# Linear-attention sums as phi(k)^T (x, 1), turned by DMA, in a kernel of two attention heads on one core

## The chip, the core and the metric

The kernel runs on one core of a Trainium2 chip. The metric is the device time of one execution in microseconds; the time of a kernel is the median of several runs. Engines are called by the names of the profile: PE (TensorE), DVE (VectorE), ACT (ScalarE), POOL (GpSimd) and SP (SyncE, which here issues every DMA). One hardware profile shows one execution, and "L287" in it is line 287 of the kernel.

## The reference, cut to what matters

Two independent blocks, A and B, on x of 2048 tokens by D = 640, with H = 32 heads of 20. A is attention over a sliding window of 256 keys. B is linear attention; the change concerns B alone:

```python
phi = lambda t: jnp.where(t > 0, t + 1, jnp.exp(t)) + 1e-6
pq, pk = phi(q), phi(k)
kv = jnp.einsum("bhsd,bhse->bhde", pk, v)
z = jnp.einsum("bhsd->bhd", pk)
num = jnp.einsum("bhqd,bhde->bhqe", pq, kv)
den = jnp.einsum("bhqd,bhd->bhq", pq, z)[..., None] + 1e-6
o = num / den        # then o @ wo; the outputs of A and B stand side by side
```

All is in bf16, with sums in f32.

## The kernel before, in words

Tokens are taken in NS = 4 blocks of SB = 512, features in KT = 5 blocks of P = 128.

**A** sets the beat. Its work is cut into 76 "tiles". A tile is a set of score products (`scores`, L763, matmul at L773) into one PSUM tile of four banks, one exponential of all of it on ACT (L793), masks on POOL (L814), and, two tiles later, the products with the values (`values`, L825, matmul at L841), whose result DVE transposes (L854), inverts (L865) and multiplies into a buffer N (L871). N has one buffer for all four blocks of tokens; four DMA transposes (`turn`, L882) carry it to oT, and the first write of the next block's N waits for them.

**B and the projections of A fill the gaps.** All other work stands as generators that yield the number of columns that each matmul streams. A plan, written by hand, gives each piece a time in tiles (`at(t0, t1, generator, n)` for chains of products, `do` for single actions), and the pieces run in the order of these times. FILL is the sum of the columns of all fill work; from it each tile gets a credit, and `take` draws that many columns of fill work between scores and values. Dense products go through four PSUM banks (`bank`, L276); `evac` (L266, its copies at L272 and L274) gives each evacuation to ACT or DVE, whichever a running account says has less to do. `soon(fn, n)` (L247) puts an action (mostly the issue of a DMA) off until n more banks have begun; `later` does so with the second half of phi on DVE (L301 and L304; its exponential on ACT is L297); chains of products (`chain`) have their matmul at L287.

**B, step by step**, with what the change touches:
- `load_tok` (L545) loads x by rows, [token, 640], into a tile of the pool `rows` (two buffers). `b_keys` (L532) makes phi(k) of 512 tokens by rows, `pk`.
- `b_sums(half)` (L550, matmul at L556) sums over the keys of half the tokens (8 blocks of 128). Because kv needs v = x wv, it suffices to know G = x^T phi(k) and to multiply by wv afterwards. x is the stationary operand, phi(k) streams. For each of 5 blocks of x's features: 8 products of 512 columns; then 5 x 8 products of 128 columns for the last 128 features of phi(k); last, z, the plain sum of phi(k): 5 x 8 products with phi(k) stationary and one column of ones streaming. The first half goes to G_acc and z_acc in f32, the second is added to it on DVE (L570 for G, L601 for z) and stored in bf16: G straight into the weights' tile `wB`, z into `zk`.
- `b_kv` (L628, matmul at L635) multiplies wv by G, by groups of six heads; `kv_ready` (L621) masks zk and kv on POOL so that each head meets its own rows alone; `b_merge` (L654, matmul at L663) multiplies kv by wo.
- `b_q(s)` (L677) makes phi(q), transposed to rows by DMA (`tok`, L694, also in the pool `rows`); `b_den(s)` (L699, L706) makes the denominators; `quotients(s)` (L732) queues four divisions on DVE (L742), each followed by a DMA transpose to `xA` (L746); one is taken a tile, by `quotient()`, in tiles that have no values, or when more than two are due, or past tile URGENT; `b_out(s)` (L750) multiplies the result by the merged matrix, after all its quotients.
- The last block of A closes the kernel: `turn_last` (L903, matmul transposes at L908, copied to oT at L914 and L916) and `a_out_last` (L918). Between the two stands what is left of the fill, the end of `b_out(3)`.

SP issues DMAs strictly in the order in which the program names them, and an issue waits on SP for what it needs.

Of the kernel before, what the change touches and what calls it, by code (L numbers as in the profile page):

```python
# [9 lines left out]
P = 128  # L10
ALU = mybir.AluOpType
ACT = mybir.ActivationFunctionType
ENG = mybir.EngineType
BF16 = mybir.dt.bfloat16
# [6 lines left out]
SB = 512  # L21
TPS = SB // P

FILL = 390760
TAIL = 13000

VALUES = 2200
TILE = 3000
COPY = 160
AHEAD = 600  # L30
URGENT = 70

# [70 lines left out]
def kernel(  # L103
# [10 lines left out]
    nc = tc.nc  # L114
    _, S, D = A_x.shape
    KT = D // P
# [13 lines left out]
    wp = pool("weights", 1)  # L130
# [10 lines left out]
    rp = pool("rows", 2)  # L141
    op = pool("o", 2)
# [9 lines left out]
    for n in "AB":  # L152
# [65 lines left out]
    NHC = GH + 2  # L218
# [28 lines left out]
    def soon(fn, banks):  # L247
        posts.append((begun[0] + banks, fn))
        posts.sort(key=lambda p: p[0])
# [16 lines left out]
    def evac(dst, src, n=SB, to=None):  # L266

        if to is None:
            to = "A" if load["A"] < load["D"] + AHEAD else "D"
        load[to] += n + COPY  # L270
        if to == "A":
            nc.scalar.activation(out=dst, in_=src, func=ACT.Copy)  # L272
        else:
            nc.vector.tensor_copy(out=dst, in_=src)  # L274

    def bank(wide=False):  # L276
        flush(begun[0] - 2)
        begun[0] += 1
        settle(False)
        if wide:  # L280
            return dps.tile([P, 2 * SB], BF16, name="dense")
        return dps.tile([P, SB], F32, name="dense")
# [49 lines left out]
    for c in range(KT):  # L332
        m = EXTRA * c
        while m < EXTRA * (c + 1):
            n = min(EXTRA * (c + 1) - m, DH - m % DH)
# [128 lines left out]
        nc.gpsimd.memset(t[:, VW:], 0.0)  # L464
    for t in v_bufs:
        nc.gpsimd.memset(t[:, :, :, DH:HV], 1.0)
    ones = wp.tile([P, 1], BF16, name="ones")
    nc.gpsimd.memset(ones[:], 1.0)
    nc.gpsimd.memset(wo_sb["B"][:, KT, :], 0.0)

    def a_v(s):
# [69 lines left out]
        yield from tok_rows(xB[s], w_sb["B"], D, done)  # L541

    x_tok = {}

    def load_tok(s):  # L545
        x_tok[s] = rp.tile([P, TPS, D], BF16, name="tok")
        src = xsrc["B"][s * SB : (s + 1) * SB, :].rearrange("(t p) d -> p t d", p=P)
        nc.sync.dma_start(out=x_tok[s], in_=src)

    def b_sums(half):  # L550
        flush()
        blocks = [(x_tok[s], pk_of[s], tb) for s in (2 * half, 2 * half + 1) for tb in range(TPS)]

        def product(out, lhs, rhs, n):
            for i, (x, pk, tb) in enumerate(blocks):
                nc.tensor.matmul(  # L556
                    out,
                    lhsT=lhs(x, pk)[:, tb, :],
                    rhs=rhs(pk, tb),
                    start=(i == 0),  # L560
                    stop=(i == len(blocks) - 1),
                )
                if i < len(blocks) - 1:
                    yield n

        def keep(at, src, n):
            if half == 0:
                evac(G_acc[at], src, n)
            else:
                nc.vector.tensor_tensor(out=G[at], in0=src, in1=G_acc[at], op=ALU.add)  # L570

        def rows(c):
            return lambda x, pk: x[:, :, c * P : (c + 1) * P]

        every = slice(None)
        for c in range(KT):
            ps = bank()
            yield from product(ps[:], rows(c), lambda pk, tb: pk[:, tb, 0:SB], SB)
            keep((every, c, slice(0, SB)), ps[:], SB)
            yield End(SB)  # L580
        for cs in (range(0, KT - 1), range(KT - 1, KT)):
            ps = bank()
            pv = ps[:].rearrange("p (c n) -> p c n", n=P)[:, 0 : len(cs), :]
            for i, c in enumerate(cs):
                yield from product(pv[:, i, :], rows(c), lambda pk, tb: pk[:, tb, SB:D], P)
                yield P
            zv = ps[:, P : P + KT]
            if len(cs) == 1:
                for c in range(KT):
                    yield from product(  # L590
                        zv[:, c : c + 1],
                        lambda x, pk: pk[:, :, c * P : (c + 1) * P],
                        lambda pk, tb: ones[:],
                        60,
                    )
            keep((every, slice(cs[0], cs[-1] + 1), slice(SB, D)), pv, len(cs) * P)
            if len(cs) == 1 and half == 0:
                nc.vector.tensor_copy(out=z_acc[:], in_=zv)
            elif len(cs) == 1:
                heads = [P, KT, NHC]  # L600
                nc.vector.tensor_tensor(  # L601
                    out=zk[:, :, :, 0],
                    in0=zv.unsqueeze(2).to_broadcast(heads),
                    in1=z_acc[:].unsqueeze(2).to_broadcast(heads),
                    op=ALU.add,
                )
            yield End(60)

    def own_heads(sgn):

# [10 lines left out]
    def kv_ready(step):  # L621

        if step == 0:
            keep_own_head(zk[:], 0, NHC, 1)
        else:
            own_heads(3 - 2 * step)

    def b_kv():  # L628

        for gs in (range(0, 4), range(4, NGR)):  # L630
            ps = bank()
            for i, g in enumerate(gs):
                w = min(GD, D - g * GD)
                for kt in range(KT):
                    nc.tensor.matmul(  # L635
                        ps[0:w, i * GD : i * GD + w],
                        lhsT=w_sb["B"][:, kt, 2 * D + g * GD : 2 * D + g * GD + w],
                        rhs=G[:, kt, g * GD : g * GD + w],
                        start=(kt == 0),
                        stop=(kt == KT - 1),  # L640
                    )
# [35 lines left out]
    def b_q(s):  # L677
        quotient(s - 2)
        xt = xB[NS + s]
        pq = pqp.tile([P, KT, SB], BF16, name="phi")  # L680
        pq_of[s] = pq
        tok = rp.tile([P, TPS, D], BF16, name="tok")
        tok_of[s] = tok
        for c in range(KT):
            ps = bank()
            yield from chain(
                ps[:],
                lambda kt: w_sb["B"][:, kt, c * P : (c + 1) * P],
                lambda kt: xt[:, kt, :],
                SB,  # L690
            )

            def to_tokens(c=c):
                nc.sync.dma_start_transpose(out=tok[:, :, c * P : (c + 1) * P], in_=pq[:, c, :])  # L694

            phi(pq[:, c, :], ps[:], then=lambda fn=to_tokens: soon(fn, 2))
            yield End(SB)
# [34 lines left out]
    def quotients(s):  # L732


        def one(tb):
            settle()
            add_load(d=1400)
            if tb == 0:
                oT_B[s] = xp.tile([P, KT, SB], BF16, name="xA")
            v = tok_of[s][:, tb, :]  # L740
            vh = v.rearrange("p (h e) -> p h e", e=DH)
            nc.vector.tensor_tensor(  # L742
                out=vh, in0=vh, in1=rden_of[s][:, tb, :, :].to_broadcast([P, H, DH]), op=ALU.mult
            )
            out = oT_B[s][:, :, tb * P : (tb + 1) * P]
            soon(lambda: nc.sync.dma_start_transpose(out=out, in_=v), 1)  # L746

        quotients_due.extend((s, tb, one) for tb in range(TPS))
# [272 lines left out]
    def at(t0, t1, gen, n):  # L1021
        for i in range(n):
            plan.append((t0 + (i + 0.5) / n * (t1 - t0), gen, i == n - 1))

    def do(t0, t1, fns):
        fns = list(fns)
        for i, fn in enumerate(fns):
            plan.append((t0 + (i + 0.5) / len(fns) * (t1 - t0), None, fn))
# [24 lines left out]
        at(t0, t1, b_sums(half), KT + 2)  # L1053
    for s, t in ((0, 6), (1, 11), (2, 24.2), (3, 28.2)):
        do(t, t, [lambda s=s: load_tok(s)])
    at(40.4, 42, b_kv(), 2)
    do(42.8, 44.8, [lambda c=c: kv_ready(c) for c in range(3)])
    for s, tq, td, tx in ((0, (39.5, 45), 46.3, 46.8), (1, (45, 50), 53, 54.3),
                          (2, (52, 57), 59.4, 60.4), (3, (58.6, 62.4), 64.9, 65.4)):
        at(*tq, b_q(s), KT)  # L1060
        at(td, td + 0.1, b_den(s), 1)
        do(tx, tx, [lambda s=s: quotients(s)])
# [102 lines left out]
```

## Time and profile before

| what | us |
|---|---|
| median of 3 runs (257.19 to 257.9) | 257.81 |
| the profiled execution, its own time | 259.17 |
| span of the profile, first to last instruction | 257.4 |
| busy: PE / ACT / DVE / POOL | 251.1 / 200.0 / 178.3 / 171.4 |
| granted PE clock | 1.000 of full speed |

The profiled execution took 1.8 us more than its span (what lies around the program), and 1.4 us more than the median. In rows of the timeline the columns are start, duration, engine, line, operation, out<-in and count; an entry in brackets is idle time of that engine before it and who ended it. A row of the waits reads "who <- for whom: total us, times, longest". A row of the windows gives the length of the stretch, then the busy time of PE, PE's weight loads, DVE, ACT and POOL (instructions in brackets), the PE clock, and the DMAs' share and rate. In the view by source line the figures are durations in ns, shortest/median/longest.

### The profile page before, as it was taken

What the parts mean: (1) busy time and instruction counts of PE and PEld (TensorE: products, weight loads), DVE (VectorE), ACT (ScalarE), POOL (GpSimd) and SP (SyncE); (2) the same over time, 40 slices, a digit from 0 to 9 for tenths busy, and PEclk for the clock granted to TensorE, in tenths of its full rate; (3) what the DMA queues carried; (4) which work ended last, traced back from release to release, by engine and by line L of the source; (5) the groups of instructions that cost most, each with busy time, mean ns of one, the idle gap of its engine ahead of it and who ended that gap; (6) DMA issues with size and microseconds to landing.
All of it is one profiled execution on the core that took longest, in us unless ns stands there. A gap on an engine that the chain in (4) does not pass through costs nothing.

```text
span 257.4 us, 10670 instructions
## 1 busy us (share of the span) xinstructions
PE 251.1 (98%) x4705; PEld 144.9 (56%) x4705; DVE 178.3 (69%) x308; ACT 200.0 (78%) x260; POOL 171.4 (67%) x211
## 2 busy tenths in 40 slices
PE   8899999999999999999999999999999999999985
PEld 7544445556556745455457655556556555555663
DVE  0345787787845456867655698599999879969552
ACT  3366888898767788897677888888889998988642
POOL 7123778876794856758495787949677695968600
PEclk9999999999999999999999999999999999999999
DMA  6997569699743152993544393642858599473905
GB/s 206 295 229 188 106 177 122 130 275 194 100 85 40 36 198 34 229 277 109 114 124 120 72 181 45 167 48 57 199 89 154 155 124 178 94 178 65 238 29 187
DMA packets 65012, 36.35 MB, mean 141 GB/s; under 512 B 48197, under 2 KB 63941, under 8 KB 64965
## 3 DMA queue, kind: packets, MB, share of 16 engines
q1 hardware_dynamic: 64965, 35.67, 64.3%
q8 instruction: 37, 0.61, 1.0%
q14 instruction: 10, 0.08, 0.1%
HBM read 14.42 MB, written 9.83 MB: 94 GB/s over the span
## 4 chain that ended last, share of the span: by engine, by line
PE 93%; DMA 5%; SPq 0%; ACT 0%; DVE 0%; issue 0%; ACTq 0%
PE dense L287 52%; PE S_ps L773 11%; PE dense L556 10%; PE dense L841 9%; PE dense L422 8%; DMA wA<-in_A_wqkv_dram 3%; DMA xA<-tok 2%; PE dense L663 1%; PE dense L706 1%; PE dense L635 1%; PE dense L188 0%; DVE wB L274 0%; SPq L968 0%; ACT vA L272 0%; SPq L182 0%
## 5 line engine op out<-in xcount | busy, mean ns | idle before, releaser
L793 ACT ACTIVATE p<-S_ps 128x2048 bf16<-128x2048 f32 x76 | 142.3, 1872 | 30.7 <-PE S_ps L773 29.6
L814 POOL TENSOR_SCALAR_AFFINE_SELECT p<-p 128x512 bf16<-128x512 bf16 (+1 forms) x152 | 122.8, 831 | 62.9 <-ACT p L793 60.5
L287 PE MATMUL dense<-xA,wqk 128*128 128x512 bf16 x200 | 50.0, 380 | 0.0
L814 POOL TENSOR_SCALAR_AFFINE_SELECT plow<-p 128x1024 bf16<-128x1024 bf16 x32 | 40.2, 1255 | 0.0
L773 PEld LDWEIGHTS <-kpad 20*128 20x128 bf16 (+1 forms) x1664 | 20.1, 97 | 26.7 <-issue 25.1
L773 PE MATMUL S_ps<-qpad,kpad 20*128 20x64 bf16 (+3 forms) x1664 | 34.5, 211 | 0.0
L854 DVE STREAM_TRANSPOSE T<-dense 128x512 f32<-128x512 f32 x32 | 22.8, 712 | 11.2 <-PE dense L841 11.1
L287 PEld LDWEIGHTS <-wqk 128*128 128x128 bf16 x200 | 18.5, 98 | 20.6 <-issue 1.3
L301 DVE TENSOR_SCALAR e<-e 128x512 bf16<-128x512 bf16 x40 | 22.5, 564 | 10.7 <-ACT e L297 9.9
L422 PE MATMUL dense<-wA,xA 128*128 128x320 bf16 x160 | 28.0, 302 | 1.1 <-DMA wA<-in_A_wqkv_dram 1.1
L304 DVE SCALAR_TENSOR_TENSOR phi<-dense,e 128x512 bf16<-128x512 f32 x40 | 27.7, 692 | 1.5
L841 PE MATMUL dense<-p,vA 128*32 128x64 bf16 (+2 forms) x1152 | 26.2, 222 | 0.0
L287 PE MATMUL dense<-wB,xB 128*128 128x512 bf16 (+1 forms) x160 | 25.9, 300 | 0.0
L287 PE MATMUL dense<-xB,wB 128*128 128x512 bf16 x100 | 25.8, 380 | 0.0
L297 ACT ACTIVATE e<-dense 128x512 bf16<-128x512 f32 x40 | 23.4, 593 | 2.9 <-PE dense L287 2.6
L287 PE MATMUL dense<-wo,oT 128*128 128x512 bf16 (+2 forms) x160 | 25.3, 300 | 0.3 <-DVE wB L274 0.3
L556 PE MATMUL dense<-phi,tok 128*128 128x512 bf16 (+1 forms) x160 | 25.1, 300 | 0.0
L287 PE MATMUL dense<-wB,xA 128*128 128x512 bf16 (+1 forms) x160 | 24.1, 300 | 0.8 <-DMA xA<-tok 0.8
L841 PEld LDWEIGHTS <-vA 128*32 128x32 bf16 x1664 | 21.6, 96 | 2.7 <-issue 0.7
L422 PEld LDWEIGHTS <-xA 128*128 128x128 bf16 x160 | 14.6, 98 | 10.0 <-issue 2.5
L272 ACT ACTIVATE osb<-dense 128x512 bf16<-128x512 f32 (+1 forms) x25 | 13.9, 571 | 7.1 <-PE dense L287 7.1
L871 DVE TENSOR_TENSOR N<-T,recA 128x320 bf16<-128x320 f32 (+1 forms) x28 | 18.6, 663 | 1.0
(68 smaller groups left out, 245.1 us busy)
## 6 DMA issues: line engine op xcount, KB each, us to landing
out_dram<-osb SPq DMA_DIRECT2D x7, 640.0 KB
x_scr<-xB SPq DMA_DIRECT2D x4, 640.0 KB
tok<-in_B_x_dram SPq DMA_DIRECT2D x4, 640.0 KB
xB<-x_scr SPq DMA_DIRECT2D x4, 640.0 KB
wB<-in_B_wqkv_dram SPq DMA_DIRECT2D x3, 800.0 KB
q_scr<-qpad SPq DMA_DIRECT2D x16, 60.0 KB
k_scr<-kpad SPq DMA_DIRECT2D x16, 60.0 KB
qpad<-q_scr SPq DMA_DIRECT2D x16, 60.0 KB
```

The lines of the kernel that those rows point to most:

```text
L287: nc.tensor.matmul(dst, lhsT=lhs(kt), rhs=rhs(kt), start=(kt == 0), stop=(kt == KT - 1))
L297: nc.scalar.activation(out=view(e), in_=src, func=ACT.Exp)
L301: nc.vector.tensor_scalar(out=e[:], in0=e[:], scalar1=1e-6, scalar2=1.0 + 1e-6, op0=ALU.add, op1=ALU.min)
L304: nc.vector.scalar_tensor_tensor(out=dst, in0=src, scalar=0.0, in1=view(e), op0=ALU.max, op1=ALU.add)
L422: nc.tensor.matmul(ps[:, 0 : hh * DH], lhsT=xt[:, kt, tb * P : (tb + 1) * P], rhs=w_sb["A"][:, kt, i * hh * DH : (i + 1) * hh * DH], start ...
L556: nc.tensor.matmul(out, lhsT=lhs(x, pk)[:, tb, :], rhs=rhs(pk, tb), start=(i == 0), stop=(i == len(blocks) - 1),)
L773: nc.tensor.matmul(columns(S_ps[0:keys], j, col, n, step), lhsT=kt[32 * j : 32 * j + DH, g, ko : ko + keys], rhs=q_pad[s][32 * j : 32 * j ...
L793: nc.scalar.activation(out=p.rearrange("p a j q -> p j a q"), in_=S_ps.rearrange("p j (a q) -> p j a q", a=2), func=ACT.Exp, scale=scale,)
L814: nc.gpsimd.affine_select(out=dst, in_=src, pattern=[[0, 4], [0, n // HALF], [sgn, HALF]], compare_op=ALU.is_ge, fill=0.0, base=base, chan ...
L841: nc.tensor.matmul(O_ps[32 * j : 32 * (j + 1), q0 : q0 + n], lhsT=v_flat[kb // TPS % 3][:, at + j * HV : at + j * HV + 32], rhs=of(p, j, c ...
L854: nc.vector.transpose(out=T.rearrange("p b e -> p (b e)"), in_=O_ps[:])
L871: nc.vector.tensor_tensor(out=dst[:, :, at : at + b - a], in0=T[:, :, a - lo : b - lo], in1=r[:].to_broadcast([P, SB // 32, b - a]), op=AL ...
```

## The change

`b_sums` changes sides: phi(k) is stationary, x streams, so the result is phi(k)^T x, with phi(k)'s features on the partitions. The tiles of rows get 16 columns more (DW = 656); column 640 is set to one on POOL, and the narrow products stream 129 columns, the last 128 features of x and the ones, so that their last column is z. The products with `ones` are gone. The narrow products come first, in two banks (3 blocks and 2), the 512-wide ones after them. In the second half the sums go to two tiles of the pool `o` (bf16), and each of the five blocks is turned into G by a DMA transpose on SP, issued one bank later. In the plan `b_kv` moves from 40.4 to 42 tiles, the masks behind it from 42.8..44.8 to 44..45.4 (the one of z to 40.5), the last `b_q` from 58.6..62.4 to 58..61.6, the last `b_den` and `quotients` by one tile, and URGENT from 70 to 68. FILL follows the columns.

```diff
-FILL = 390760
+FILL = 386520
...
-URGENT = 70
+URGENT = 68
...
-    ones = wp.tile([P, 1], BF16, name="ones")
-    nc.gpsimd.memset(ones[:], 1.0)
...
+    DW = D + 16
+    def rows_tile():
+        return rp.tile([P, TPS, DW], BF16, name="tok")
     def load_tok(s):
-        x_tok[s] = rp.tile([P, TPS, D], BF16, name="tok")
+        x_tok[s] = rows_tile()
...
-        nc.sync.dma_start(out=x_tok[s], in_=src)
+        nc.sync.dma_start(out=x_tok[s][:, :, 0:D], in_=src)
+        nc.gpsimd.memset(x_tok[s][:, :, D : D + 1], 1.0)
     def b_sums(half):
...
+        if half:
+            turned = [op.tile([P, TPS, D], BF16, name="osb") for _ in range(2)]
+        def product(out, c, lo, hi):
             for i, (x, pk, tb) in enumerate(blocks):
                 nc.tensor.matmul(
                     out,
-                    lhsT=lhs(x, pk)[:, tb, :],
-                    rhs=rhs(pk, tb),
+                    lhsT=pk[:, tb, c * P : (c + 1) * P],
+                    rhs=x[:, tb, lo:hi],
...
+        def keep(c, lo, hi, src):
             if half == 0:
-                evac(G_acc[at], src, n)
+                evac(G_acc[:, c, lo:hi], src, hi - lo)
             else:
-                nc.vector.tensor_tensor(out=G[at], in0=src, in1=G_acc[at], op=ALU.add)
+                nc.vector.tensor_tensor(
+                    out=turned[c // TPS][:, c % TPS, lo:hi],
+                    in0=src,
+                    in1=G_acc[:, c, lo:hi],
+                    op=ALU.add,
+                )
...
+        for cs in (range(0, 3), range(3, KT)):
+            ps = bank()
+            pv = ps[:, 0 : len(cs) * (P + 1)].rearrange("p (c n) -> p c n", n=P + 1)
+            for i, c in enumerate(cs):
+                yield from product(pv[:, i, :], c, SB, D + 1)
...
+            for i, c in enumerate(cs):
+                keep(c, SB, D, pv[:, i, 0:P])
+            zv = pv[:, :, P]
...
         for c in range(KT):
             ps = bank()
-            yield from product(ps[:], rows(c), lambda pk, tb: pk[:, tb, 0:SB], SB)
-            keep((every, c, slice(0, SB)), ps[:], SB)
+            yield from product(ps[:], c, 0, SB)
+            keep(c, 0, SB, ps[:])
+            if half:
+                def turn(c=c):
+                    nc.sync.dma_start_transpose(
+                        out=G[:, :, c * P : (c + 1) * P], in_=turned[c // TPS][:, c % TPS, :]
+                    )
+                soon(turn, 1)
             yield End(SB)
-        for cs in (range(0, KT - 1), range(KT - 1, KT)):
...
-                    yield from product(
-                        zv[:, c : c + 1],
-                        lambda x, pk: pk[:, :, c * P : (c + 1) * P],
-                        lambda pk, tb: ones[:],
-                        60,
-                    )
...
-    at(40.4, 42, b_kv(), 2)
-    do(42.8, 44.8, [lambda c=c: kv_ready(c) for c in range(3)])
+    do(40.5, 40.5, [lambda: kv_ready(0)])
+    at(42, 43.4, b_kv(), 2)
+    do(44, 45.4, [lambda c=c: kv_ready(c) for c in (1, 2)])
     for s, tq, td, tx in ((0, (39.5, 45), 46.3, 46.8), (1, (45, 50), 53, 54.3),
-                          (2, (52, 57), 59.4, 60.4), (3, (58.6, 62.4), 64.9, 65.4)):
+                          (2, (52, 57), 59.4, 60.4), (3, (58, 61.6), 63.9, 64.4)):
```

`b_q` takes its tile of rows from `rows_tile` too, and the quotients read its first 640 columns.

More of the change, by code (lines that the diff above doesn't have):

```diff
@@ L552, in b_sums @@
         blocks = [(x_tok[s], pk_of[s], tb) for s in (2 * half, 2 * half + 1) for tb in range(TPS)]
-        def product(out, lhs, rhs, n):
+        every = slice(None)
+        if half:
+            turned = [op.tile([P, TPS, D], BF16, name="osb") for _ in range(2)]
+        def product(out, c, lo, hi):
             for i, (x, pk, tb) in enumerate(blocks):
@@ L563, in product @@
                 if i < len(blocks) - 1:
-                    yield n
-        def keep(at, src, n):
+                    yield hi - lo
+        def keep(c, lo, hi, src):
             if half == 0:
-                evac(G_acc[at], src, n)
+                evac(G_acc[:, c, lo:hi], src, hi - lo)
             else:
[L570 to L575, printed above, removed]
+                nc.vector.tensor_tensor(
[4 more added lines that the diff above has]
+                )
@@ new lines, in b_sums @@
+        for cs in (range(0, 3), range(3, KT)):
[3 more added lines that the diff above has]
+                yield from product(pv[:, i, :], c, SB, D + 1)
+                if i < len(cs) - 1:
+                    yield P + 1
+            for i, c in enumerate(cs):
+                keep(c, SB, D, pv[:, i, 0:P])
+            zv = pv[:, :, P]
+            at = slice(cs[0], cs[-1] + 1)
+            if half == 0:
+                nc.vector.tensor_copy(out=z_acc[:, at], in_=zv)
+            else:
+                heads = [P, len(cs), NHC]
+                nc.vector.tensor_tensor(
+                    out=zk[:, at, :, 0],
+                    in0=zv.unsqueeze(2).to_broadcast(heads),
+                    in1=z_acc[:, at].unsqueeze(2).to_broadcast(heads),
+                    op=ALU.add,
+                )
+            yield End(P + 1)
@@ L576, in b_sums @@
         for c in range(KT):
             ps = bank()
-            yield from product(ps[:], rows(c), lambda pk, tb: pk[:, tb, 0:SB], SB)
-            keep((every, c, slice(0, SB)), ps[:], SB)
-            yield End(SB)
-        for cs in (range(0, KT - 1), range(KT - 1, KT)):
[L582 to L589, printed above, removed]
-                    yield from product(
-                        zv[:, c : c + 1],
-                        lambda x, pk: pk[:, :, c * P : (c + 1) * P],
-                        lambda pk, tb: ones[:],
-                        60,
-                    )
[L596 to L607, printed above, removed]
@@ L609, in own_heads @@
+            yield from product(ps[:], c, 0, SB)
[4 more added lines that the diff above has]
+                        out=G[:, :, c * P : (c + 1) * P], in_=turned[c // TPS][:, c % TPS, :]
+                    )
+                soon(turn, 1)
+            yield End(SB)
     def own_heads(sgn):
@@ L681, in b_q @@
         pq_of[s] = pq
-        tok = rp.tile([P, TPS, D], BF16, name="tok")
+        tok = rows_tile()
         tok_of[s] = tok
@@ L739, in one @@
                 oT_B[s] = xp.tile([P, KT, SB], BF16, name="xA")
-            v = tok_of[s][:, tb, :]
+            v = tok_of[s][:, tb, 0:D]
             vh = v.rearrange("p (h e) -> p h e", e=DH)
```

## The prediction

> **What bounds the kernel now.** I read the page first: the busy shares, the slices and the chain that ended last.
>
> ```profile
> span 257.4 us, 10670 instructions
> ...
> PE 251.1 (98%) x4705; PEld 144.9 (56%) x4705; DVE 178.3 (69%) x308; ACT 200.0 (78%) x260; POOL 171.4 (67%) x211
> ...
> PE   8899999999999999999999999999999999999985
> ...
> PE 93%; DMA 5%; SPq 0%; ACT 0%; DVE 0%; issue 0%; ACTq 0%
> ```
>
> TensorE is full in every slice between the start and the last few microseconds, and the chain runs through it for 93% of the span. So whatever is taken out of TensorE's stream in the middle comes off the time one for one, as long as nothing starts to wait in its place. Next, the view of waits for TensorE alone, leaving out the loads at the start:
>
> ```profile
> PE dense L287 <- DMA xA<-tok: 0.8, 1, 0.8
> PE dense L287 <- DVE wB L274: 0.3, 1, 0.3
> ```
>
> Behind the start there are only two waits: one for a turned `xA<-tok` (the last quotient of B), one for an evacuation by VectorE. The first is what the second half of the change aims at; the change does not touch what the second waits for.
>
> **The change part by part.**
>
> *The sums with `ones` go.* Two stretches of the timeline hold all 80 of these products.
>
> ```profile
> 87.66 0.49 PE L556 MATMUL dense<-ones,phi 128*128 128x1 bf16 x14
> 88.09 0.40 PE L773 MATMUL S_ps<-qpad,kpad 20*128 20x256 bf16 x8
> 88.42 0.80 PE L556 MATMUL dense<-ones,phi 128*128 128x1 bf16 x26
> 89.08 0.84 PE L422 MATMUL dense<-wA,xA 128*128 128x320 bf16 x5
> ```
> ```profile
> 136.46 0.62 PE L556 MATMUL dense<-phi,tok 128*128 128x128 bf16 x8
> ...
> 136.92 1.14 PE L556 MATMUL dense<-ones,phi 128*128 128x1 bf16 x40
> ...
> 137.92 0.38 PE L287 MATMUL dense<-xA,wqk 128*128 128x512 bf16 x1
> ```
>
> Matmuls overlap, so their price is from start to start, not their duration. First half: 14 products from 87.66 to 88.09 and 26 from 88.42 to 89.08, 0.43 + 0.66 = 1.09 us. Second half: 40 from 136.92 to 137.92, 1.00 us. Together **2.09 us** leave TensorE, some 26 ns each. In their place the narrow products grow from 128 columns to 129: 8 of them took 136.92 - 136.46 = 0.46 us, 57 ns each, so a 129th column is 0.45 ns, times 80: +0.04 us. The number of 512-wide products, and their price, stay; the operands only change sides.
>
> *Narrow sums first.* The column blocks that need the last phi(k) now come at once, not after 40 wide products.
>
> ```profile
> 117.00 0.81 PE L556 MATMUL dense<-phi,tok 128*128 128x512 bf16 x3
> ...
> 117.50 0.69 DVE L304 SCALAR_TENSOR_TENSOR phi<-dense,e 128x512 bf16<-128x512 f32 x1
> ...
> 118.11 0.68 DVE L274 CAST kpad<-dense 128x512 bf16<-128x512 f32 x1
> 118.11 2.55 PE L556 MATMUL dense<-phi,tok 128*128 128x512 bf16 x11
> ...
> 119.34 0.69 DVE L304 SCALAR_TENSOR_TENSOR phi<-dense,e 128x512 bf16<-128x512 f32 x1
> ...
> 120.59 0.40 PE L773 MATMUL S_ps<-qpad,kpad 20*128 20x192 bf16 x16
> ```
>
> With the sums of the second half starting at 117.00, the seventh narrow product (117.00 + 6 x 0.057 = 117.34) needs the phi that ended at 118.19: up to 0.85 us late. The fifth block, 26 products on (118.19 + 1.48 = 119.67, and the scores between), needs the phi that ended at 120.03, about when it is there. In the new order one evacuation of VectorE (`kpad`, 0.68 us) moves from ahead of those phis to between them, which takes most of the wait away. Bounds 0 and 0.85; I take **+0.3 us** for both halves together.
>
> *G is turned by DMA.* Five DMA transposes are new, each 128 x 640, the size of `xA<-tok` at L746. SP and the DMAs carry them, not TensorE; they cost something only if `b_kv` has to wait.
>
> ```profile
> 138.10 0.29 DVE L570 TENSOR_TENSOR wB<-dense,wo 128x128 bf16<-128x128 f32 x1 [0.81 <-PE dense L556]
> ```
> ```profile
> L570 DVE TENSOR_TENSOR wB<-dense,wo x7: 292/690/692, 119.9 to 138.1; 128x512 bf16<-128x512 f32 x6, 128x128 bf16<-128x128 f32 x1
> ```
> ```profile
> 140.67 0.55 PE dense L635 x10
> ...
> 241.62 4.96 DMA xA<-tok
> ```
>
> Before, the first product of `b_kv` (L635) followed the last sum of G by 2.3 us (138.39 to 140.67). A transpose took 4.96 us from issue to landing at its slowest on the chain, so there it would have stood still. The change moves `b_kv` 1.4 to 1.6 tiles back, and the order of instructions of the changed kernel puts 28 products of 512 columns, two tiles of scores and a group of values between the last sum and `b_kv`. At 225 ns a product (11 of them from 118.11 to 120.59, above) the 28 alone are 6.3 us, against 0.69 us for the sum (L570) and 4.96 for the transpose: hidden, with about a microsecond to spare and the tiles on top. I cost it at nothing; without that cover it would be up to 3 us.
>
> *SP's queue.* The transposes of G stand on SP between those of A's output (L882), and each waits for its sum on VectorE.
>
> ```profile
> SPq L548 <- PE dense L556: 10.0, 1, 10.0
> ```
> ```profile
> 127.13 2.91 SPq L882 DMA_TRANSPOSE oT<-N  x2
> ```
> ```profile
> 138.69 0.65 DVE L871 TENSOR_TENSOR N<-T,recA 128x320 bf16<-128x320 f32 x1
> ```
>
> The first row shows SP held for 10.0 us by one load, with all that is queued behind it. Before, the last two `oT<-N` went out by 127.13 + 2.91 = 130.04, and the next write of their source N came at 138.69. The order now has those two behind the fourth transpose of G, four fifths through the sums of the second half (117.00 to 138.10): its sum is due near 132 to 134, three issues at 1.46 us follow, and 5 us to land: 139 to 142. The write of N then waits 0 to 3 us, and VectorE with it.
>
> ```profile
> 132.00:138.00 6.00, 6.00 (x167) 4.70 (x165) 2.79 (x4) 3.92 (x4) 4.55 (x7) 1.00 0.21 52
> ```
>
> VectorE (the fourth figure) was idle for over half of 132 to 138, and what TensorE needs from it next in the new order, an evacuation and a phi, stands some 4 us of products further on. I take 0 for TensorE, with 1 us as the upper end. [...]
>
> *Small change on VectorE and GpSimd.* Five narrow evacuations a half at 0.29 us (the shortest of L570) stand for one of 0.69 and one of 0.29: +0.5 us a half, and one more tiny z copy, off TensorE's path while VectorE has idle time; bounds 0 and the 0.5. On GpSimd four memsets of one column replace one; the masks of p that TensorE needs stand behind them, but it is busy for 67% only. Nothing, up to some tenths.
>
> *The last quotients a tile sooner.*
>
> ```profile
> 235.90 0.40 PE L773 MATMUL S_ps<-qpad,kpad 20*128 20x256 bf16 x8
> ```
> ```profile
> 241.62 2.40 SPq L746 DMA_TRANSPOSE xA<-tok  x1
> ...
> 244.79 1.07 PE L908 MATMUL dense<-ident,N 128*128 128x128 bf16 x16
> ...
> 246.62 1.59 PE L287 MATMUL dense<-wB,xA 128*128 128x512 bf16 x11 [0.77 <-DMA xA<-tok]
> 247.09 0.65 DVE L916 COPY oT<-dense 128x1024 bf16<-128x1024 bf16 x1
> ```
> ```profile
> 248.83 5.60 PE L287 MATMUL dense<-wo,oT 128*128 128x320 bf16 x40
> ```
>
> The 16 turns of L908 end at 244.79 + 16 x 0.057 = 245.70; the next product waits for the transpose issued at 241.62 until 246.62: 0.92 us. In the new order that transpose stands beside the last scores but one (before, those at 235.90), 5 us sooner, and the wait goes. What is late next is the copy of oT (L916), which ends 247.74 - 244.79 = 2.95 us after the turns begin. TensorE gets there, with 4 products of 512 (0.22 each) and 20 of 128 (0.057) left between, after 0.91 + 0.88 + 1.14 = 2.93 us. So it waits some 0.1 us instead of 0.92: **-0.8 us**.
>
> **Sum** against the profiled execution: 257.4 - 2.09 + 0.04 + 0.3 - 0.8 = 254.85 in span, and 259.17 - 2.55 = 256.6 with the 1.8 us around it. The median of the runs, 257.81, stands 1.4 below the profiled time, so the forecast is 257.81 - 2.55, **255.3 us**.
>
> **Rivals.**
>
> *The gain at the end does not come, or waits eat part of it:* the late phi at its bound (+0.55 over the sum) and the end still held by a transpose (+0.8), or 1 us behind the write of N: 256 to 257. For it: oT's copy is only 0.1 us from being the bound. Against: the transpose gets some 5 us.
>
> *Slower: VectorE becomes the bound ahead of the end.* Chains of phi(q) and quotients move from its idle time into its fullest stretch.
>
> ```profile
> 210.00:216.00 6.00, 6.00 (x184) 3.39 (x175) 4.89 (x9) 5.61 (x9) 4.75 (x7) 1.00 0.77 149
> 216.00:222.00 6.00, 6.00 (x94) 2.77 (x83) 5.90 (x10) 5.64 (x10) 4.04 (x4) 1.00 0.84 140
> 222.00:228.00 6.00, 6.00 (x135) 3.91 (x133) 5.57 (x10) 5.71 (x8) 5.93 (x7) 1.00 0.62 102
> ```
> ```profile
> L742 DVE TENSOR_TENSOR tok<-tok,rden 128x640 bf16<-128x640 bf16 x11 | 13.6, 1237 | 0.0
> L304 DVE SCALAR_TENSOR_TENSOR phi<-dense,e 128x512 bf16<-128x512 f32 x14 | 9.7, 692 | 0.5
> L301 DVE TENSOR_SCALAR e<-e 128x512 bf16<-128x512 bf16 x14 | 7.2, 518 | 1.9 <-ACT e L297 1.6
> ```
>
> VectorE has 1.11 + 0.10 + 0.43 = 1.64 us idle between 210 and 228. One quotient (1.24) and one phi (0.69 + 0.52) moved in are 2.45, 0.8 too much, and the banks have slack for part of that. If all five phis (6.05) came into it, 4.4 us would be over and TensorE would wait for banks: 255.3 + 4.4 = 259.7. It turns slower than before once over 4.2 us come in. Against: the plan moves these by 0.6 to 1 tile only.
>
> *The transposes of G arrive late,* held on SP: `b_kv` would wait up to 3 us, 255.3 + 3 = 258.3, no change to be seen. Decided by whether the last lands later than the 28 products allow.
>
> **How the numbers follow.** About 0.3% (0.8 us) is what a measurement of this kernel tells from no change. The forecast (254.2 to 256.0, its low end without the late phi and the 0.3 us wait for `wB`, and by the scatter of the runs) has 0.62; the smaller gain (256 to 257) 0.2; G late or the like 0.08; VectorE as the bound 0.1. So faster 0.82, same 0.08, slower 0.10. The range 254.2 to 257.2 takes in the first two.
>
> **What would show it.** Right: no `dense<-ones,phi`; TensorE still full from 10 us on; its wait for `xA<-tok` gone, and the copy of oT ending about when TensorE reaches `wo,oT`; `b_kv` without a wait for a DMA. Wrong: a wait of TensorE for `wB<-osb`, for phi of more than 0.9 us in the sums, for banks held by VectorE between 205 and 230, or an end that still waits for `xA<-tok`.

## The result, and the profile after

| | median, us | ratio to before, 95% interval |
|---|---|---|
| before, 7 runs | 257.90 (257.19 to 258.59) | 1 |
| after, 7 runs | 256.37 (256.05 to 257.07) | 0.9943 (0.9923 to 0.9962) |
| after, once more, 12 runs beside 35 of before | 256.23 (255.58 to 258.28) | 0.9930 (0.9908 to 0.9952) |

The change gains 1.5 to 1.8 us. The forecast was 2.55; its sign and most of its terms hold, its size does not. The median of 256.37 lies in the stated range of 254.2 to 257.2, but above the forecast's own 254.2 to 256.0. Single runs of the changed kernel lie up to 2.7 us apart.

The page of the changed kernel, its head:

```profile
span 254.6 us, 10488 instructions
...
PE 244.4 (96%) x4578; PEld 142.9 (56%) x4625; DVE 181.6 (71%) x315; ACT 199.2 (78%) x261; POOL 170.7 (67%) x214
...
PE   8999999999999999999999999999999999999995
...
PE 90%; issue 4%; DVE 4%; ACT 1%; ACTq 0%
```

PE has 4625 weight loads but only 4578 products on record. The 47 others are missing from this trace, and each leaves an apparent hole of some 0.2 us. The second profile of the same kernel has all of them, and its slices are as full as before. Its waits of PE are all of this view:

```profile
PE dense L422 <- DMA wA<-in_A_wqkv_dram: 1.1, 1, 1.1
PE dense L207 <- DVE osb L203: 1.1, 1, 1.1
PE dense L853 <- ACT p L779: 0.3, 1, 0.3
```

The waits for `xA<-tok` and for `wB`, both in the view of before, are gone. The first two rows belong to the start, which is not of one length: A's first exponential comes at 19.48 us in the profile of before, at 18.20 and 20.61 in the two of after, at 17.7 to 18.5 in the others. I therefore split every profile at the first and the last exponential of A, `p<-S_ps`. First before, then after:

```profile
19.48 1.88 ACT L793 ACTIVATE p<-S_ps 128x2048 bf16<-128x2048 f32 x1 [0.74 <-PE S_ps L773]
...
239.12 1.88 ACT L793 ACTIVATE p<-S_ps 128x2048 bf16<-128x2048 f32 x1
```
```profile
18.20 1.88 ACT L805 ACTIVATE p<-S_ps 128x2048 bf16<-128x2048 f32 x1 [0.74 <-PE S_ps L785]
...
237.11 1.88 ACT L805 ACTIVATE p<-S_ps 128x2048 bf16<-128x2048 f32 x1 [0.86 <-PE S_ps L785]
```

The body, between them, took 219.64 us before and 218.91 after: 0.73 less. The end, from the last exponential to the last instruction, took 18.25 and 17.53: 0.72 less. By the sum on record the body should have given 1.75 (2.09 - 0.04 - 0.3) and the end 0.8. The end came as forecast; a microsecond is missing in the body.

Where it went is read from PE's starts. I took the time from the start of each product to the start of the next, and compared it with the median of the same pair of shapes; three places of the body stand out. In the timeline of after:

```profile
141.77 0.50 PE L785 MATMUL S_ps<-qpad,kpad 20*128 20x64 bf16 x34
...
142.71 0.24 PE L785 MATMUL S_ps<-qpad,kpad 20*128 20x64 bf16 x6 [0.44 <-issue]
```
```profile
177.38 0.68 DVE L274 CAST osb<-dense 128x512 bf16<-128x512 f32 x1
...
178.12 0.51 PE L853 MATMUL dense<-p,vA 128*32 128x256 bf16 x16
```
```profile
198.62 0.62 ACT L272 ACTIVATE osb<-dense 128x512 bf16<-128x512 f32 x1
...
199.29 0.21 PE L853 MATMUL dense<-plow,vA 128*32 128x64 bf16 x4 [0.27 <-ACT p L779]
```

The first is a halt in the middle of a tile of scores, between its 34th and its 35th product, with nothing waited for: 0.62 us over the usual step. In the second and third, values need one of the four PSUM banks, and start 0.05 us after an evacuation has ended (178.06, 199.24): 0.19 and 0.34 us. The view names ACT's L779 in the third, which had just ended too (199.10 + 0.19). None of the three is in the trace of before.

### The profile page after: what moved, and what is told of

It reads as the page before. It is cut to its first block, busy times and chain, and to the rows that moved or that the text cites. A ratio compares the mean times of both kernels' runs of the same rounds, so it can differ in the third digit from the quotient of the medians.

```text
span 254.6 us, 10488 instructions
## 1 busy us (share of the span) xinstructions
PE 244.4 (96%) x4578; PEld 142.9 (56%) x4625; DVE 181.6 (71%) x315; ACT 199.2 (78%) x261; POOL 170.7 (67%) x214
## 4 chain that ended last, share of the span: by engine, by line
PE 90%; issue 4%; DVE 4%; ACT 1%; ACTq 0%
PE dense L287 48%; PE S_ps L785 11%; PE dense L853 9%; PE dense L564 9%; PE dense L422 9%; PE dense L207 1%; DVE phi L304 1%; PE dense L718 1%; ACT e L297 1%; PE dense L188 1%; PE dense L675 1%; PE dense L647 1%; DVE tok L754 1%; DVE e L301 1%; ACT osb L272 0%
## 5 line engine op out<-in xcount | busy, mean ns | idle before, releaser
L287 PE MATMUL dense<-xA,wqk 128*128 128x512 bf16 x188 | 48.9, 380 | 1.3 <-issue 0.8
L826 POOL TENSOR_SCALAR_AFFINE_SELECT plow<-p 128x1024 bf16<-128x1024 bf16 x32 | 40.4, 1261 | 0.0
L301 DVE TENSOR_SCALAR e<-e 128x512 bf16<-128x512 bf16 x40 | 23.6, 590 | 13.2 <-ACT e L297 13.0
L287 PEld LDWEIGHTS <-wqk 128*128 128x128 bf16 x200 | 17.9, 98 | 20.6 <-issue 2.3
L422 PE MATMUL dense<-wA,xA 128*128 128x320 bf16 x160 | 26.5, 303 | 0.2 <-issue 0.2
L287 PE MATMUL dense<-wo,oT 128*128 128x128 bf16 (+2 forms) x155 | 24.5, 297 | 0.5 <-issue 0.2
L287 PE MATMUL dense<-xB,wB 128*128 128x512 bf16 x90 | 24.4, 380 | 0.5 <-issue 0.3
L564 PE MATMUL dense<-tok,phi 128*128 128x129 bf16 (+1 forms) x152 | 23.9, 296 | 0.9 <-issue 0.8
L287 PE MATMUL dense<-wB,xA 128*128 128x128 bf16 (+1 forms) x152 | 22.8, 295 | 0.7 <-issue 0.5
L883 DVE TENSOR_TENSOR N<-T,recA 128x320 bf16<-128x320 f32 (+1 forms) x28 | 19.6, 698 | 2.7 <-DMA oT<-N 1.8
L272 ACT ACTIVATE osb<-dense 128x512 bf16<-128x512 f32 (+1 forms) x26 | 14.6, 571 | 7.6 <-PE dense L287 7.1
```

The lines of the kernel that those rows point to most:

```text
L287: nc.tensor.matmul(dst, lhsT=lhs(kt), rhs=rhs(kt), start=(kt == 0), stop=(kt == KT - 1))
L301: nc.vector.tensor_scalar(out=e[:], in0=e[:], scalar1=1e-6, scalar2=1.0 + 1e-6, op0=ALU.add, op1=ALU.min)
L422: nc.tensor.matmul(ps[:, 0 : hh * DH], lhsT=xt[:, kt, tb * P : (tb + 1) * P], rhs=w_sb["A"][:, kt, i * hh * DH : (i + 1) * hh * DH], start ...
L564: nc.tensor.matmul(out, lhsT=pk[:, tb, c * P : (c + 1) * P], rhs=x[:, tb, lo:hi], start=(i == 0), stop=(i == len(blocks) - 1),)
L826: nc.gpsimd.affine_select(out=dst, in_=src, pattern=[[0, 4], [0, n // HALF], [sgn, HALF]], compare_op=ALU.is_ge, fill=0.0, base=base, chan ...
L883: nc.vector.tensor_tensor(out=dst[:, :, at : at + b - a], in0=T[:, :, a - lo : b - lo], in1=r[:].to_broadcast([P, SB // 32, b - a]), op=AL ...
```

## The experiments

Body and end as above, from one profile each; ratios from the times, against before on the same chip.

| kernel | ratio, 95% interval | median, us | body, us | end, us | halts of PE without a wait, us |
|---|---|---|---|---|---|
| before | 1 | 257.9 to 258.4 | 219.64 | 18.25 | none over 0.15 |
| after | 0.9943 (0.9923 to 0.9962) | 256.37 | 218.91 | 17.53 | 0.62 |
| again | 0.9930 (0.9908 to 0.9952) | 256.23 | 218.45 | 17.52 | none over 0.25 |
| ones_back | 1.0039 (1.0014 to 1.0063) | 259.34 | 220.41 | 17.52 | none |
| ones_half | 0.9997 (0.9976 to 1.0018) | 258.02 | 220.52 | 17.52 | 0.41, 0.59 |
| end_back | 1.0002 (0.9981 to 1.0023) | 258.41 | 219.65 | 19.32 | 0.88, 0.47 |
| end_back_take | 0.9932 (0.9909 to 0.9956) | 256.77 | 219.25 | 17.37 | 0.33 |
| end_only | 0.9972 (0.9952 to 0.9992) | 257.58 | 221.41 | 17.30 | 1.18, 0.43 |
| kv_early | 0.9946 (0.9920 to 0.9971) | 256.23 | 218.51 | 17.54 | none |
| kv_take | 0.9936 (0.9912 to 0.9961) | 256.58 | 218.33 | 17.39 | none |
| wo_early (other numbers, see below) | 1.0105 (1.0070 to 1.0139) | 260.77 | 222.95 | 17.52 | 3.07 |
| wo_swap | 1.0088 (1.0056 to 1.0120) | 260.28 | 223.80 | 17.52 | 2.77 |

**again**: no edit.

> The changed kernel once more, for a second profile. Its trace shows 1.3 us of waits of TensorE that the kernel before does not have: 0.62 in the middle of a tile of scores at 142.1 us with nothing waited for, 0.19 at 178.1 and 0.34 at 199.3 ahead of values, each for a PSUM bank that an evacuation frees late, and 0.11. Theory 'made by the order': all three stand at the same instructions again, 0.5 to 0.7, 0.1 to 0.3 and 0.2 to 0.4 us, and the time is 1.3 to 1.8 us under before. Rival 'accidents of one execution': at least the 0.62, which no semaphore explains, is gone or stands elsewhere.

Both theories hold a part. The waits for banks are back at the same products (180.06 and 201.23 in a span that began 1.95 us later), 0.19 and 0.34 us: the order makes them. The 0.62 is gone, and the body is 0.46 shorter: an accident of one execution, at least in whether it comes.

**ones_back** (in `b_sums`, behind each narrow chain):

```diff
                 yield from product(pv[:, i, :], c, SB, D + 1)
+                for j, (x, pk, tb) in enumerate(blocks):
+                    nc.tensor.matmul(
+                        ps[:, 400 + i : 401 + i],
+                        lhsT=pk[:, tb, c * P : (c + 1) * P],
+                        rhs=x[:, tb, D : D + 1],
+                        start=(j == 0),
+                        stop=(j == len(blocks) - 1),
+                    )
```

> The changed kernel with 80 products of one column put back behind the narrow ones, 8 to a chain, phi(k) stationary and the column of ones streaming into columns of the bank that nothing reads; all else in its old order. Theory 'priced from start to start': 80 x 26 ns = 2.1 us more than the changed kernel, about 258.4. Rival 'they lay beside other work' (weight loads, or the waits for phi at the start of the sums take them in): under 1.2 us more.

The body grew from 218.45 (again, also without a halt) to 220.41: 1.96 us, 24.5 ns a product. The times differ by more, 2.8 us by the ratios, each of which is uncertain by 0.6. The profiled execution was the fastest of the twelve (257.72, median 259.34); what made the others longer no trace shows. The price of 26 ns holds in the traces; the rival, under 1.2, falls by traces and times.

**ones_half**: the same, `enumerate(blocks if half == 0 else [])`.

> The changed kernel with the 40 one-column products put back behind the narrow ones of the first half alone. Theory 'priced from start to start': 40 x 26 ns = 1.0 us over the changed kernel, 257.3, half of what the 80 cost. The same kernel moves every later block of 256 instructions by 80 places: theory 'TensorE waits for its own instructions' has any stall without a semaphore again 194 or 195 instructions into a block, so at other products than those of 142.1 us; rival 'something in that tile' has it in the same tile.

The body is 220.52; less its two halts (0.41 and 0.59) it is 219.52, 1.07 over again: half of the price. The halts stand at other products than in after, one of them in the sums. What that tells is taken up below.

**end_back** and **end_only**: the plan's last row and URGENT, alone.

```diff
-                          (2, (52, 57), 59.4, 60.4), (3, (58, 61.6), 63.9, 64.4)):
+                          (2, (52, 57), 59.4, 60.4), (3, (58.6, 62.4), 64.9, 65.4)):
...
-URGENT = 68
+URGENT = 70
```

> The changed kernel with the last phi(q) chains, denominators and quotients, and URGENT, at the times of before. Theory 'the end is worth 0.8, and the waits are not its doing': the wait of 0.8 to 0.9 us for the last transpose of quotients is back, 0.8 over the changed kernel, 257.2. Rival 'the moved chains pay for it': the wait of 0.34 at 199.3 goes as it comes, 0.4 to 0.5 over the changed kernel, 256.8. Third: more than 0.8 over it, up to 257.9, if the sums' part is worth nothing.

> The kernel before with nothing changed but the last phi(q) chains, denominators and quotients, and URGENT, at the times of after. Theory 'the end is worth 0.8': 257.9 - 0.8 = 257.1, no wait for xA at the end, a wait of 0.1 for the copy of oT in its place. Rival 'the moved chains pay': the same, and a new wait of 0.2 to 0.4 ahead of values near 200 us: 257.4.

end_only gives 0.7 us (0.2 to 1.2) in the times and 0.95 at the end of its trace: the end is worth about what was forecast. (Its body is 1.77 longer than that of before; 1.61 of that are two halts.) It has no new wait ahead of values near 200 us, and end_back still has its 0.34 there: the moved chains do not pay. But end_back is no faster than before at all. In its trace, two halts of 1.35 us together take what the body gained. And its end is 1.79 longer than that of after, about as much as the times differ (1.5 to 1.9), and 1.07 longer than that of before (19.32 against 18.25). The timeline shows why:

```profile
239.98 1.96 SPq L758 DMA_TRANSPOSE xA<-tok  x1
```
```profile
239.23 2.98 PE L287 MATMUL dense<-wB,xA 128*128 128x512 bf16 x13
243.81 0.39 PE L287 MATMUL dense<-wB,xA 128*128 128x512 bf16 x1 [1.60 <-DMA xA<-tok]
...
244.93 1.07 PE L920 MATMUL dense<-ident,N 128*128 128x128 bf16 x16
245.83 1.36 PE L287 MATMUL dense<-wB,xA 128*128 128x512 bf16 x10
```

Before, the product that needs the last transpose came behind the 16 turns. Here it stands ahead of the last values: with the new FILL and columns per product, one product more has slipped into the columns drawn there, and the 1.7 us of values and turns that had covered most of the wait come after it.

**end_back_take**: end_back, and in the loop over the last values

```diff
-        take(5500)
+        take(5000)
```

> The changed kernel with the last phi(q), denominators, quotients and URGENT at the times of before, as in end_back, and the columns drawn ahead of the last values cut from 5500 to 5000, so that 5 products of 512 stand behind the last turns, as in the kernel before, and not 4. In end_back one product, the first that needs the last transpose of quotients, had slipped ahead of the last values and the turns, and the wait was 1.76 instead of 0.92. Theory 'the sums' gain was lost in that one product': the wait stands behind the turns again, 0.7 to 1.0, and the time is 0.8 under end_back, 257.6. Rival 'the last transpose itself is what holds the end': TensorE gets there sooner by what the sums saved, the wait grows as before to 1.6 or more, and the time stays at 258.4.

The loss was in that one product, but neither theory has the number: the wait is not 0.7 to 1.0, it is gone.

```profile
240.37 1.67 SPq L758 DMA_TRANSPOSE xA<-tok  x1
```
```profile
243.33 1.07 PE L920 MATMUL dense<-ident,N 128*128 128x128 bf16 x16
244.24 2.36 PE L287 MATMUL dense<-wB,xA 128*128 128x512 bf16 x24
```

The last transpose was issued at 240.37 here, in end_back it took 3.8 us to land (239.98 to 243.81), and PE comes to it at 244.24, just behind that. In before the same transpose took 4.96 us; by an estimate from these rows (240.37 + 4.96 = 245.33), PE would with that have waited 1.1 us here too. So the wait is gone because the transpose landed sooner; why it did was not tried. With the sums alone and this one number the whole gain is there in the times (ratio 0.9932), and the earlier quotients are one of two ways to it. What 5000 columns would give the kernel before was not run.

**kv_early**:

```diff
-    at(42, 43.4, b_kv(), 2)
+    at(40.4, 42, b_kv(), 2)
```

> The changed kernel with b_kv back at the plan's time of before (40.4 to 42): 10 products of 512 columns and one tile of scores are left between the last sum of G and b_kv, 2.5 us, where the changed kernel has 30 and more. Theory 'the transposes of G are hidden by the distance alone': the last turn (issued 135.66 in the changed kernel, 2.5 to 5 us to land) is now 1 to 3.3 us late, TensorE waits for DMA wB<-osb that long, and the time grows by as much, 257.3 to 259.6. Rival 'they would have been in time': a wait of under 0.5 us, time unchanged.

The rival holds. In its timeline, SP first, then PE:

```profile
132.06 1.21 SPq L614 DMA_TRANSPOSE wB<-osb  x1
133.32 2.64 SPq L894 DMA_TRANSPOSE oT<-N  x2
136.06 1.25 SPq L614 DMA_TRANSPOSE wB<-osb  x1
```
```profile
136.28 1.25 PE L287 MATMUL dense<-xB,wB 128*128 128x512 bf16 x5
137.37 1.26 PE L647 MATMUL dense<-wB 128*120 128x120 bf16 x20
```

`b_kv` starts 0.06 us after the issue of the fifth transpose has ended, and waits for nothing. Its first bank multiplies four groups of heads, columns 0 to 479 of G, and these come from the first four transposes; the fourth went out at 132.06, 5.3 us earlier. The fifth is needed only by the second bank, which starts at 143.73.

**wo_early**: A's output weights at 25.8 in place of 40.6. They share a tile with the running sums G_acc, so here they are loaded over them and overwritten by them: B's G and A's output weights are both other numbers, while every instruction keeps its form.

> The changed kernel with one thing moved: the 15 loads of A's output weights go out at tile 25.8 (some 92 us, SP and DMAs idle) instead of tile 40.6. TensorE, VectorE, ScalarE and GpSimd keep their instructions in the same order; SP's alone changes. Theory 'TensorE waits for its own instructions': the stall in the scores at 142.1 us (0.62 and 0.88 in two profiles, none in a third) stands 194 instructions into a block of 256, and ended 1.3 us after a fetch of 16,384 bytes that had started late among those loads. With the DMAs free there the fetch comes in time: no stall at that place, none over 0.2 at 140 to 145 us, and the time 0.2 to 0.5 under the changed kernel, 256.0. Rival 'something else in that tile': the stall can come back, and the time is the same.

The halt did not go. It grew to 3.07 us, at the very same product:

```profile
141.79 0.50 PE L785 MATMUL S_ps<-qpad,kpad 20*128 20x64 bf16 x34
145.18 0.23 PE L785 MATMUL S_ps<-qpad,kpad 20*128 20x64 bf16 x6 [2.89 <-issue]
```

The expectation was wrong on what the edit does to the DMAs. With A's 15 loads out of the way, SP came sooner to what stood behind them: B's output weights, one issue of 750 KB, went out at 137.25 and not at 144.12. The DMAs were some 80% busy from 138 to 146 us. That suggests the opposite test, with A's output weights behind B's and all numbers right:

**wo_swap**:

```diff
-(40.6, "A", A_wo), (42, "B", B_wo)
+(40.5, "B", B_wo), (40.6, "A", A_wo)
```

> The changed kernel with the load of B's output weights (one issue of 750 KB and one of 50) ahead of the 15 loads of A's, not behind them. Nothing else moves: TensorE, VectorE, ScalarE and GpSimd keep their instructions in the same order. The DMAs are then busier at 137 to 142 us, when the block of instructions that holds the scores of 142.1 us is fetched. Theory 'TensorE waits for its own instructions, and DMA traffic makes the fetch late': the fetch starts over 2 us behind its usual place, the stall stands at the same product, 194 instructions into the block, and is 1 to 3 us; the time grows by 0.7 to 2 us over the changed kernel, 257 to 258.5. Rival 'the stall has nothing to do with DMA': 0 to 0.9 us there, as in the changed kernel, and the same time.

Met in the trace: 34 products, then a halt of 2.77 us at the same place, and only SP's order had changed. The packet of instructions started at 141.66 (140.27 in after). The time grew by 3.9 us, more than the 0.7 to 2 expected and more than the halt; the windows show the rest (behind POOL's figure stands the granted clock):

```profile
141.43 0.50 PE L785 MATMUL S_ps<-qpad,kpad 20*128 20x64 bf16 x34
144.51 0.29 PE L785 MATMUL S_ps<-qpad,kpad 20*128 20x64 bf16 x6 [2.59 <-issue]
```
```profile
138.00:142.00 4.00, 3.93 (x140) 2.22 (x138) 3.84 (x8) 3.05 (x6) 3.42 (x6) 1.00 0.95 204
142.00:146.00 4.00, 1.49 (x10) 0.61 (x11) 2.36 (x3) 1.16 (x1) 2.06 (x2) 0.71 0.72 156
146.00:150.00 4.00, 4.00 (x33) 2.73 (x32) 1.81 (x4) 1.40 (x3) 2.92 (x3) 0.50 0.32 68
150.00:154.00 4.00, 4.00 (x95) 2.31 (x91) 1.15 (x4) 2.64 (x3) 1.28 (x2) 0.94 0.72 114
```

The granted clock was 0.50 from 146 to 150 us, 0.71 in the 4 us before and 0.94 in the 4 after; as an estimate from these three, it stood at half for some 7 us (2.3 + 4 + 0.5), most of it after the halt. The body is 5.35 over that of again: 2.77 for the halt, and 2.6 more, which I put down to the clock. The profiled execution (260.89, mean clock 0.987) is above the median of 260.28; of the five others one has 0.987, three 0.993 and one 1.000.

**kv_take**: after, with kv_early's and end_back_take's lines.

> The changed kernel with b_kv at the time of before (as in kv_early, where it waited for nothing) and 5000 columns drawn ahead of the last values in place of 5500 (as in end_back_take, where the copy of oT was no longer late). Expected: no wait for wB<-osb, none for xA or oT at the end (0.13 less than the changed kernel), no stall at the block of 142 us; 255.9 to 256.2, at or a little under the changed kernel. The rival, that one of the two only held with the rest as it was: a new wait of 0.3 or more, 256.5.

The trace is as expected: no halt, no wait at the end, and the shortest body and end together of all profiles (235.72 from the first exponential, against 235.97 in again). The times (256.58, 0.9936) cannot tell it from the changed kernel.

### The halts: PE waits for its own instructions

The DMA view of the changed kernel has a queue of its own for instructions:

```profile
q8 instruction: 36, 0.59, 1.0%
```

36 packets for 0.59 MB are 16,384 bytes each. PE's program has 9,276 instructions (4625 weight loads, as many products, 26 others); that is 258 to a packet. I take 256 to each, 64 bytes an instruction, an estimate from these two figures. Counting in program order, all ten halts over 0.3 us, in seven kernels, stand at the same place of such a block: 194 or 195 instructions after a multiple of 256 (5058 in after, end_back, end_back_take, wo_early and wo_swap; 6851 in end_back; 4034 in end_only and ones_half; 2243 in ones_half; 8898 in end_only). In each case a packet had ended 1.2 to 1.6 us before PE went on (after: 140.27 + 1.15 = 141.42, PE on at 142.70). ones_half, whose 40 products shift the blocks by 80 instructions, has its halts in other tiles, and in the sums, but at 194 and 195 again.

The packets come late when the DMAs are busy. Over 399 packets of the 12 traces I took the time from PE's 192nd instruction of a block to the start of the packet that follows: 0.63 us in the mean and 1.2 at most where the DMAs were under 10% busy in the 2 us around, 1.9 in the mean and 4.7 at most where they were over 100% (packets overlap). Most blocks last 5 to 9 us, more than any of these times. A block that holds a tile of scores of 40 products and a group of values lasts 3.1 to 4 us, and one of these lies at 139 to 142 us in the changed kernel, among the loads of the output weights; before, the block there lasted 5.2. So the change, by taking out 160 instructions, moved the borders of the blocks, and put a short one where the DMAs are 57% busy (138 to 142 us).

The packet's end also tells which blocks halt. I took the time from there to PE's 190th instruction of the next block: it is under 1.2 us at all ten halts and at one other place (1.06 in again, where 0.21 us are lost). Wherever it was 1.2 us or more, no halt over 0.3 followed.

The new order is not alone in this. end_only has the blocks of before and halts twice, the second time in a chain of products:

```profile
233.44 1.46 PE L287 MATMUL dense<-wB,xA 128*128 128x512 bf16 x6
235.16 1.25 PE L287 MATMUL dense<-wB,xA 128*128 128x512 bf16 x5 [0.26 <-issue]
```

In the trace of before the packets of the same two blocks had ended 1.4 and 1.5 us ahead, just in time. How often each kernel halts, and which loses more by it, single traces do not tell.

## Why the prediction was partly wrong

- **The 80 products with ones, -2.09**: right. Put back, they cost 1.96 in the body; half of them, 1.07.
- **The late phi, +0.3**: not there in that form. The seventh narrow product starts on time in both halves. One narrow product of the first half is late, by 0.15 us: the 25th, the first of the second bank, at 65.38, when the phi of 64.64 + 0.69 has ended. It reads a phi(k) that products since 63.19 had read already; so it does not wait for that phi's result, but most likely for the PSUM bank that the same instruction reads (this is argued from the kernel's order, not tried). Six of the ten traces with the new sums have this wait, again has not.

```profile
63.19 1.52 PE L564 MATMUL dense<-tok,phi 128*128 128x129 bf16 x24
...
64.55 0.84 PE L422 MATMUL dense<-wA,xA 128*128 128x320 bf16 x5
65.38 0.56 PE L564 MATMUL dense<-tok,phi 128*128 128x129 bf16 x7
```
```profile
64.64 0.69 DVE L304 SCALAR_TENSOR_TENSOR phi<-dense,e 128x512 bf16<-128x512 f32 x1
```

- **G's transposes, 0**: right, for a reason that was not the one given. "Without that cover it would be up to 3 us" is wrong: without it (kv_early) it is 0, because the first bank needs four transposes of five.
- **SP's queue, 0 on PE with the write of N 0 to 3 us late**: right; the write was 1.79 us late, and PE waited for nothing that came of it.

```profile
137.57 0.49 DVE L883 TENSOR_TENSOR N<-T,recA 128x320 bf16<-128x320 f32 x1 [1.79 <-DMA oT<-N]
```

- **The end, -0.8**: right in size (0.72), and in what is late next. The copy of oT ends at 245.84, and PE's first product with it starts at 245.90, 0.13 late:

```profile
242.88 1.07 PE L920 MATMUL dense<-ident,N 128*128 128x128 bf16 x16
244.00 1.93 PE L287 MATMUL dense<-wB,xA 128*128 128x512 bf16 x23
245.90 1.26 PE L287 MATMUL dense<-wo,oT 128*128 128x320 bf16 x8
```
```profile
245.19 0.65 DVE L928 COPY oT<-dense 128x1024 bf16<-128x1024 bf16 x1
```

  That it adds to the rest was luck: the forecast took the two gains as separate, and without the earlier quotients the sums' gain is lost to one product at the end (end_back).
- **What failed** is the first step: "whatever is taken out of TensorE's stream in the middle comes off the time one for one, as long as nothing starts to wait in its place". The sum had no term for new waits ahead of values, nor for halts. That was 0.53 us for banks, in every trace with the new sums, and 0.62 for instructions in the profiled execution. The body without a long halt (again) gained 1.19 of 1.75; the two waits are 0.53 of the 0.56 that lack. That these agree so closely is partly chance, for other terms of both signs lie beside them: a halt of 0.21 in again, and the wait for `wB`, 0.3 in the view of before and in no view of after, though the prediction said that the change does not touch what it waits for. With the sizes that again shows, the body comes to 1.96 - 0.04 + 0.3 - 0.53 - 0.21 = 1.48 against 1.19, and 0.3 us has no place. Why the new sums make just these two waits, 40 us and more behind them, was not tried and stays open.
- **The rivals**: the measured 256.37 lies in the case of the smaller gain, but by neither mechanism that it named; that the stated range held it is luck to that extent. VectorE did not become the bound: no wait of PE for it between 205 and 230 us in the second profile.

## What to carry to other kernels

Work taken out of a full engine is gained only after the new order has been read for waits: a hand-kept plan that counts columns shifts every piece behind the edit, and one product drawn ahead of its cover can cost the whole gain (end_back, 1.0002, against end_back_take, 0.9932). When an engine halts with nothing to wait for, count its instructions and look at the DMA queue for instructions; then keep large loads away from short, instruction-rich stretches (with a load of 750 KB moved ahead of such a stretch, in wo_swap, the halt there was 2.77 us, against 0.62 in after and none in again). A dependency on five transfers is to be split by what each consumer reads of them.

## What the runs showed of the hardware

- PE's 9,276 instructions in after came by DMA in 36 packets of 16,384 bytes, some 258 to each. Ten times, in seven kernels, PE stood still for 0.33 to 3.07 us with nothing else waited for, each time 194 or 195 instructions behind a multiple of 256, and went on 1.2 to 1.6 us after a packet had ended. The packets started 0.63 us after PE's 192nd instruction, in the mean, where the DMAs were under 10% busy, and 1.9 where they were over 100%.
- In wo_swap, with a halt of 2.77 us, TensorE's granted clock was 0.50 from 146 to 150 us, and the body grew by 2.6 us more than the halt; in wo_early, with one of 3.07 us, the clock was 0.57 in the mean from 146 to 150 us and 1.00 from 150 to 154. In end_back, with a wait of 1.60 us, it was 1.00 throughout 236 to 248 us.
- The start varies by itself: A's first exponential came 17.7 to 20.6 us after the first instruction in twelve profiles. Differences of the body are better read from the first exponential on.
